# Weight sums paced through the first network, attention traced between its matmuls, split second weights kept by the first token group, block sums in PSUM

## The chip, the cores and the metric

The kernel runs on one core of a Trainium2 chip. The metric is the device time of the whole program in microseconds (us); lower is better. Five engines work side by side: TensorE (PE; its weight loads are PEld), VectorE (DVE), ScalarE (ACT), GpSimd (POOL) and SyncE (SP), which issues most DMAs. Each engine runs its own instructions in a fixed order and waits on semaphores for the others.

## What is computed

```python
attn = masked_softmax(q @ k.T / 8)          # 4 batches, 8 heads, 576 tokens, head size 64
x = (attn @ v) -> (2304, 512)               # window of 32, plain or with dilation 4
xn = x / rms(x) * rms_g                     # first network, width 1536
x = (silu(xn @ w_gate) * (xn @ w_val)) @ w_out
P = sinkhorn(exp(x @ gate2))                # (2304, 8), 8 rounds over rows and columns
for e in range(8):                          # second network, 8 experts, width 1024
    out += P[:, e:e+1] * (relu(x @ w1[e]) @ w2[e])
```

All of it is fp32. The kernel splits each matmul operand into a high part and a remainder (hi, lo) and multiplies hi*hi, hi*lo and lo*hi, so each product takes three matmul passes.

## The kernel before, in words

**First network.** The 2304 tokens are eight blocks of 256 or 320. For a block, `block_att` runs its attention tiles of 128 tokens: scores on PE, softmax on DVE and ACT, then a norm whose power -1/2 is taken on POOL (`rstd`, line 292), then transposes (`psXT`) that give `xn`. `gemm_h` makes one of twelve slices of the hidden layer: PE fills `pg` and `pv`, ACT, DVE and POOL make `h` (lines 473 to 476). `gemm_out` multiplies by `w_out` and stores to `x2d` in HBM. The weights are first unpacked and split on ACT, DVE and POOL (`split_double`, lines 358 to 380); this is done by about 232 us.

**Sums.** The second network multiplies 2x2 blocks with seven products in place of eight (Winograd's form), so it needs sums of weight blocks. `weight_sums` makes them in 64 items, one for each half of `w1` and of `w2` for each of 16 chunks: SP loads 512 KB into one of three buffers (`kbd`, `vbd`, `conv`), one DVE and three POOL operations add blocks, SP stores 512 KB to `sums`. For blocks 2 to 7, `spread` interleaves a side generator with the matmul generators at fixed ratios.

**Second network.** 48 units: three token groups `g` of 768 tokens times 16 chunks (expert and half of its width). A unit has seven steps `s`; step by step, `gemm1(u)` (12 matmuls of 384 columns) alternates with `gemm2(u-1)` (18 matmuls of 256 columns), so a unit of time has 84 + 126 = 210 matmuls. `gemm1` accumulates in three chains of PSUM banks, a, c and b, two banks each out of four: b takes the banks that c leaves, and the next unit's a those that b leaves. After its steps, ACT copies block sums out (`p1`, `pq`, `u4`), DVE adds a bank to them, `direct` makes the hidden blocks a11, a22 and a12 (`h_a`: ACT relu, DVE remainder), and `relu_with` makes four more sums (line 872). `summed` turns those into s2, s4, s3 and s1 (`h_s`: ACT cast, POOL remainder) in the next unit. `gemm2` multiplies the `h` blocks by the split weights and DVE adds the result to `acc`, scaled by the routing weight (line 963).

During unit u, `second_weights(u)` loads four tiles for `w2` (two raw, two of sums) and splits seven blocks (`w_b`, `w_t`: ACT cast, the remainder on DVE for four and on POOL for three), and `first_weights(u+1)` does the same for `w1` (`w_a`, `w_s`, all on POOL). All of them come out of one pool of 20 buffers. This is done anew in each of the three groups, though the weights are the same.

Ahead of the last unit's end of a group, `x_load` and `x_split` prepare the next group's tokens. In units 0 to 2 a side generator does the last gate (`gate`, line 543 on PE) and the Sinkhorn rounds. Instructions stand on an engine in the order that a scheduler in the build makes of the trace order; SP's DMAs are in order too.

## Time and profile before

| | |
|---|---|
| median of three runs | 2268.74 us (2268.07 to 2269.47) |
| profiled execution, its own time | 2270.99 us |
| its span, first to last instruction | 2269.2 us |
| mean granted TensorE clock | 0.960 |
| PE / PEld busy | 2073.0 / 2016.4 us (91%, 89%) |
| DVE / POOL / ACT busy | 1625.0 / 1509.0 / 1135.2 us |

Busy time of PE is the time in which a matmul is in the array, its pipelined end modelled, so 99% is not peak. The idle time of PE and of PEld, and what ended it, tell more. The clock of 1.00 is 2.4 GHz.

### The profile page before, as it was taken

How to read it: one execution, taken by the hardware profiler on the slowest of the kernel's cores; microseconds unless marked ns; L12 is line 12 of the kernel's file. 1: busy time of each engine (PE TensorE's matmuls, PEld its weight loads, DVE VectorE, ACT ScalarE, POOL GpSimd, SP SyncE). 2: the span in 40 equal slices, each digit the busy share in tenths (PEclk: the TensorE clock that was granted, in tenths of full speed). 3: DMA queues.
4: the chain of work that ended last, by engine and by line, in shares of the span. 5: the costliest groups of instructions: out<-in, count | busy, mean ns of one | idle time of the engine just before them, and what ended most of it. 6: DMA issues, size and time to landing. Idle time of an engine off the chain costs nothing.

```text
span 2269.2 us, 42225 instructions
## 1 busy us (share of the span) xinstructions
PE 2073.0 (91%) x16098; PEld 2016.4 (89%) x16098; DVE 1625.0 (72%) x3000; ACT 1135.2 (50%) x2444; POOL 1509.0 (66%) x1351
## 2 busy tenths in 40 slices
...
GB/s 271 170 227 191 269 258 266 174 177 27 53 89 158 91 124 124 130 144 149 149 137 115 143 128 138 140 150 148 124 129 148 121 131 149 149 132 122 128 140 65
DMA packets 161034, 333.48 MB, mean 147 GB/s; under 512 B 12352, under 2 KB 20160, under 8 KB 160832
## 3 DMA queue, kind: packets, MB, share of 16 engines
...
q8 instruction: 126, 2.06, 0.4%
q14 instruction: 76, 0.62, 0.1%
HBM read 287.76 MB, written 42.99 MB: 146 GB/s over the span
## 4 chain that ended last, share of the span: by engine, by line
POOL 23%; PE 22%; DMA 20%; DVE 12%; issue 11%; ACT 4%; POOLq 0%; SPq 0%; DVEq 0%; ACTq 0%
DMA w0r<-in_w 12%; POOL h_s L868 7%; POOL w_a L620 5%; POOL w_s L620 5%; PE ya L935 4%; PE pa L888 3%; PE po L435 3%; PE pv L461 3%; PE pg L461 3%; DVE h_a L860 2%; PE yb L935 2%; DVE w_b L620 2%; POOL w_t L620 2%; DVE acc L963 2%; POOL w_b L620 2%
## 5 line engine op out<-in xcount | busy, mean ns | idle before, releaser
L620 POOL TENSOR_TENSOR w_s<-w0s,w_s 128x512 fp32r<-128x512 f32 x192 | 291.9, 1530 | 12.0 <-ACT w_s L619 12.0
L620 POOL TENSOR_TENSOR w_a<-w0r,w_a 128x512 fp32r<-128x512 f32 x144 | 203.9, 1417 | 141.7 <-ACT w_a L619 126.2
L868 POOL TENSOR_TENSOR h_s<-p,h_s 128x384 fp32r<-128x384 f32 x96 | 125.5, 1323 | 235.1 <-ACT h_s L867 227.7
L963 DVE SCALAR_TENSOR_TENSOR acc<-ya,Pm,acc 128x256 f32<-128x256 f32 x534 | 231.5, 473 | 19.3 <-PE ya L935 16.2
L935 PE MATMUL ya<-w_t,h_s 128*128 128x256 f32 x1728 | 228.6, 285 | 5.9 <-DVE acc L963 5.4
L935 PEld LDWEIGHTS ya<-w_t,h_s 128*128 128x128 f32 x1728 | 222.9, 193 | 7.9 <-DVE acc L963 5.8
L888 PE MATMUL pa<-x_t,w_s 128*128 128x384 f32 x1152 | 223.2, 340 | 3.4 <-ACT p L900 2.4
L461 PE MATMUL pv<-xn,w_v 128*128 128x320 f32 (+1 forms) x1152 | 192.4, 313 | 22.3 <-POOL w_v L374 7.6
L888 PEld LDWEIGHTS pa<-x_t,w_s 128*128 128x128 f32 x1152 | 200.9, 192 | 4.5 <-ACT p L900 2.7
L461 PEld LDWEIGHTS pv<-xn,w_v 128*128 128x128 f32 x1152 | 173.7, 203 | 27.6 <-POOL w_v L374 8.0
L619 ACT CAST w_t<-w1s 128x512 fp32r<-128x512 f32 x192 | 119.0, 621 | 157.5 <-POOL w_s L620 89.5
L461 PE MATMUL pg<-xn,w_g 128*128 128x320 f32 (+1 forms) x1152 | 187.5, 305 | 8.8 <-DVE hf L474 5.7
L435 PE MATMUL po<-h,w_o 128*128 128x320 f32 (+1 forms) x1152 | 182.2, 306 | 7.8 <-DVE partial L446 2.9
L620 DVE TENSOR_TENSOR w_t<-w1s,w_t 128x512 fp32r<-128x512 f32 x96 | 121.2, 1262 | 81.5 <-ACT w_t L619 81.4
L461 PEld LDWEIGHTS pg<-xn,w_g 128*128 128x128 f32 x1152 | 168.4, 196 | 12.4 <-DVE hf L474 6.1
L435 PEld LDWEIGHTS po<-h,w_o 128*128 128x128 f32 x1152 | 165.5, 195 | 12.6 <-DVE partial L446 3.8
L619 ACT CAST w_s<-w0s 128x512 fp32r<-128x512 f32 x192 | 119.2, 621 | 108.0 <-POOL w_a L620 74.5
L476 POOL TENSOR_TENSOR h<-hf,h 128x256 fp32r<-128x256 f32 (+1 forms) x96 | 82.6, 864 | 113.6 <-ACT h L475 113.4
L935 PE MATMUL yb<-w_t,h_s 128*128 128x256 f32 x864 | 131.3, 294 | 21.7 <-POOL h_s L868 21.5
L935 PEld LDWEIGHTS yb<-w_t,h_s 128*128 128x128 f32 x864 | 115.8, 194 | 34.3 <-POOL h_s L868 33.6
L860 DVE SCALAR_TENSOR_TENSOR h_a<-p,h_a 128x384 fp32r<-128x384 f32 x96 | 90.5, 947 | 62.6 <-ACT h_a L859 57.9
L620 POOL TENSOR_TENSOR w_t<-w1s,w_t 128x512 fp32r<-128x512 f32 x96 | 131.7, 1372 | 2.4 <-ACT w_t L619 2.4
(235 smaller groups left out, 5191.7 us busy)
## 6 DMA issues: line engine op xcount, KB each, us to landing
...
```

The costliest lines, as they stand in the source:

```text
L435: nc.tensor.matmul(po[:, :n], lhsT=ow[f][:, a, dc * P : dc * P + P], rhs=hs[blk, f][:, bb, :n], start=k == 0, stop=k == 11,)
L461: nc.tensor.matmul(ps[:, :n], lhsT=w[kt, fg][:, a, fo * P : fo * P + P], rhs=xn[:, kt, bb, :n], start=k == 0, stop=k == 11,)
L476: nc.gpsimd.tensor_tensor(out=h[:, 1, :n], in0=hf, in1=h[:, 0, :n].bitcast(F32), op=ALU.subtract)
L619: nc.scalar.copy(v[:, :, 0, :], src)
L620: lo_eng.tensor_tensor(out=v[:, :, 1, :], in0=src, in1=v[:, :, 0, :].bitcast(F32), op=ALU.subtract)
L860: nc.vector.scalar_tensor_tensor(out=h[:, 1, :], in0=src, scalar=0.0, in1=h[:, 0, :].bitcast(F32), op0=ALU.max, op1=ALU.subtract)
L868: nc.gpsimd.tensor_tensor(out=h[:, 1, :], in0=src, in1=h[:, 0, :].bitcast(F32), op=ALU.subtract)
L888: nc.tensor.matmul(ps, lhsT=w1s[u, a][:, kt, hl, q * P : q * P + P], rhs=xc[b, kt][:, xl, :TH], start=fresh and k == 0, stop=k == 5, skip_ ...
L935: nc.tensor.matmul(ps, lhsT=hh[u, a, q][:, hl, jj * P : jj * P + P], rhs=w2s[u, b][:, q, wl, :], start=fresh and k == 0 and jj != 1, stop= ...
L963: nc.vector.scalar_tensor_tensor(out=dst, in0=ps, scalar=scale, in1=dst, op0=ALU.mult, op1=ALU.add)
```

## The change

Four parts, in the order of the program:

1. `weight_sums` yields twice for each item, is asked for 24 steps in each of blocks 2 to 7 in place of 13, and its additions stand behind the newest `hf` and `h` operations of `gemm_h` on DVE and POOL. `block_att(i+1)` is no longer run ahead of block i's matmuls but is a side generator of their `spread`.
2. `last_gate` takes the place of the last `gate`: all four token tiles are loaded and split first, into tiles of the `h` pool, and the matmuls come five steps later.
3. In group 0, each split `w2` block is also stored to HBM (`split2`, 512 KB). In groups 1 and 2, `second_weights` loads the seven blocks from there and neither loads raw `w2` and its sums nor splits.
4. In `gemm1`, the additions for a11 (step 1) and a12 (step 5) are written back into their PSUM bank, `direct` reads that bank, and ACT copies the sum to `p1` or `pq` afterwards. In step 6 the relu is written into its own bank and two `relu_with` read it there.

```diff
@@ -471,10 +471,11 @@
         h = mpool.tile([P, 2, 320], F32R, tag="h", name=f"h_{blk}_{f}", bufs=5)
         hf = mpool.tile([P, 320], F32, tag="hf", name=f"hf_{blk}_{f}", bufs=2)[:, :n]
         nc.scalar.activation(hf, pg[:, :n], AF.Silu)
-        nc.vector.tensor_tensor(out=hf, in0=pv[:, :n], in1=hf, op=ALU.mult)
+        late_v = nc.vector.tensor_tensor(out=hf, in0=pv[:, :n], in1=hf, op=ALU.mult)
         nc.scalar.copy(h[:, 0, :n], hf)
-        nc.gpsimd.tensor_tensor(out=h[:, 1, :n], in0=hf, in1=h[:, 0, :n].bitcast(F32), op=ALU.subtract)
+        late_g = nc.gpsimd.tensor_tensor(out=h[:, 1, :n], in0=hf, in1=h[:, 0, :n].bitcast(F32), op=ALU.subtract)
         hs[blk, f] = h
+        marks["late"] = (late_v, late_g)
         yield
 
     pending = []
@@ -565,6 +566,8 @@
         for w in range(2) for ch in range(NCH)
     }
 
+    split2 = [dram.tile([7, P, 1024], F32, name=f"split2_{ch}", tag=f"split2_{ch}") for ch in range(NCH)]
+
     def raw_of(w, ch):
         e, c = divmod(ch, 2)
         return w1[e, :, 512 * c : 512 * c + 512] if w == 0 else w2[e, 512 * c : 512 * c + 512, :]
@@ -584,6 +587,10 @@
         yield
         for i, (w, ch, k) in enumerate(items):
             nxt = load(i + 1) if i + 1 < len(items) else None
+            yield
+            late = ExitStack()
+            for m in marks["late"]:
+                late.enter_context(tc.issue_after(m.ins))
             x11, x12, x21, x22 = (t[:, a, 256 * c : 256 * c + 256] for a in range(2) for c in range(2))
             if w == 0:
                 nc.gpsimd.tensor_tensor(out=x22, in0=x12, in1=x22, op=ALU.add)
@@ -595,6 +602,7 @@
                 nc.vector.tensor_tensor(out=x12, in0=x22, in1=x12, op=ALU.subtract)
                 nc.gpsimd.tensor_tensor(out=x22, in0=x11, in1=x22, op=ALU.subtract)
                 nc.gpsimd.tensor_tensor(out=x21, in0=x21, in1=x22, op=ALU.add)
+            late.close()
             nc.sync.dma_start(sums[w, ch][:, k, :], t.rearrange("p i n -> p (i n)"))
             t = nxt
             yield
@@ -618,7 +626,7 @@
         v = t.rearrange("p k (s n) -> p k s n", s=2)
         nc.scalar.copy(v[:, :, 0, :], src)
         lo_eng.tensor_tensor(out=v[:, :, 1, :], in0=src, in1=v[:, :, 0, :].bitcast(F32), op=ALU.subtract)
-        return v
+        return t, v
 
     def first_weights(u):
 
@@ -626,19 +634,27 @@
         yield
         yield
         for m, src in (("a11", a11), ("a12", a12), ("s2", s2), ("s3", s3), ("s1", s1), ("a22", a22), ("s4", s4)):
-            w1s[u, m] = split_block(f"w1_{u}_{m}", src, nc.gpsimd)
+            w1s[u, m] = split_block(f"w1_{u}_{m}", src, nc.gpsimd)[1]
             yield
 
     def second_weights(u):
 
+        g, ch = units[u]
+        names = ("b11", "b21", "t2", "t3", "t1", "t4", "b22")
+        if g > 0:
+            for j, m in enumerate(names):
+                t = wx.tile([P, 2, 512], F32R, tag="w", name=f"w2_{u}_{m}")
+                nc.sync.dma_start(t.rearrange("p k n -> p (k n)").bitcast(F32), split2[ch][j])
+                w2s[u, m] = t.rearrange("p k (s n) -> p k s n", s=2)
+                yield
+            return
         b11, b12, b21, b22, t1, t3, t4, t2 = blocks_of(1, u)
         yield
         yield
         yield
-        for j, (m, src) in enumerate(
-            (("b11", b11), ("b21", b21), ("t2", t2), ("t3", t3), ("t1", t1), ("t4", t4), ("b22", b22))
-        ):
-            w2s[u, m] = split_block(f"w2_{u}_{m}", src, nc.gpsimd if j % 2 else nc.vector)
+        for j, (m, src) in enumerate(zip(names, (b11, b21, t2, t3, t1, t4, b22))):
+            t, w2s[u, m] = split_block(f"w2_{u}_{m}", src, nc.gpsimd if j % 2 else nc.vector)
+            nc.sync.dma_start(split2[ch][j], t.rearrange("p k n -> p (k n)").bitcast(F32))
             yield
 
 
@@ -787,12 +803,14 @@
     ready = {2: (0,), 3: (1,), 4: (2,), 6: (3,)}
     sgen1 = weight_sums()
     for i in range(2, 8):
+        sides = [(some(sgen1, 24), 24)]
         if i < 7:
-            run(block_att(i + 1))
-            spread(moe1_chunks([(i, 0), (i, 1), (i, 2)]), 34, [(some(sgen1, 13), 13), *((later(g), 34) for g in ready.get(i, ()))])
+            sides.append((block_att(i + 1), 7 * len(blocks[i + 1][2])))
+            sides += [(later(g), 34) for g in ready.get(i, ())]
         else:
-            run(sgen1)
-            spread(moe1_chunks([(i, 0), (i, 1), (i, 2)]), 34, [(tail(), 34), (later(4), 34)])
+            sides += [(tail(), 34), (later(4), 34)]
+        spread(moe1_chunks([(i, 0), (i, 1), (i, 2)]), 34, sides)
+    run(sgen1)
 
     ph1.close()
     psum_a.close()
@@ -807,9 +825,42 @@
     ones = acp.tile([P, P], F32, name="ones")
     nc.gpsimd.memset(ones, 1.0)
 
+    def last_gate():
+
+        blk = NT // TH - 1
+        xg = [hp_.tile([P, 2, TH], F32R, tag="h", name=f"xg_{kt}") for kt in range(4)]
+        for kt in range(4):
+            st = stg.tile([P, 512], F32, tag="st", name=f"sx_{blk}_{kt}", bufs=3)[:, :TH]
+            nc.sync.dma_start(st, x2d[kt, :, TH * blk : TH * blk + TH])
+            nc.scalar.copy(xg[kt][:, 0, :], st)
+            nc.gpsimd.tensor_tensor(out=xg[kt][:, 1, :], in0=st, in1=xg[kt][:, 0, :].bitcast(F32), op=ALU.subtract)
+            if kt % 2:
+                yield
+        for _ in range(5):
+            yield
+        pl = ps_o.tile([P, 512], F32, tag="o", name="pl_last")
+        for k in range(8):
+            kt, hl = divmod(k, 2)
+            nc.tensor.matmul(
+                pl[:16, :TH], lhsT=wg[:, kt].rearrange("p s e -> p (s e)"), rhs=xg[kt][:, hl, :], start=k == 0, stop=k == 7
+            )
+        yield
+        lg = stg.tile([16, 512], F32, tag="st", name="lg_last", bufs=3)
+        nc.scalar.copy(lg[:, :TH], pl[:16, :TH])
+        for _ in range(2):
+            yield
+        ptl = ps_o.tile([P, 512], F32, tag="o", name="ptl_last")
+        nt = TH // P
+        for j in range(nt):
+            nc.tensor.transpose(ptl[:, j * 16 : j * 16 + 16], lg[:, j * P : j * P + P], id16)
+        nc.vector.tensor_copy(
+            L2[:, nt * blk : nt * blk + nt, :], ptl[:, : nt * 16].rearrange("p (t e) -> p t e", e=16)
+        )
+        yield
+
     def side():
 
-        yield from gate(NT // TH - 1)
+        yield from last_gate()
         nc.vector.tensor_tensor(out=Pm, in0=L2[:, :, 0:8], in1=L2[:, :, 8:16], op=ALU.add)
         gm = acp.tile([P, 2], F32, name="gm")
         nc.vector.tensor_reduce(out=gm[:, 0:1], in_=Pm.rearrange("p t e -> p (t e)"), axis=AX.X, op=ALU.max)
@@ -898,17 +949,22 @@
                     tag = {0: "p1", 2: "pq", 4: "u4"}[s]
                     t[tag, q] = temp(tag, u, q)
                     nc.scalar.copy(t[tag, q], ps)
-                if s in (1, 4, 5):
-                    m, tag, src = {1: ("a11", "p1", "c"), 4: ("a22", "u4", "b"), 5: ("a12", "pq", "b")}[s]
+                if s in (1, 5):
+                    m, tag = {1: ("a11", "p1"), 5: ("a12", "pq")}[s]
                     x = t[tag, q]
-                    nc.vector.tensor_tensor(out=x, in0=bank[src, q][:, :TH], in1=x, op=ALU.add)
-                    direct(u, m, q, x)
+                    nc.vector.tensor_tensor(out=ps, in0=ps, in1=x, op=ALU.add)
+                    direct(u, m, q, ps)
+                    nc.scalar.copy(x, ps)
+                if s == 4:
+                    x = t["u4", q]
+                    nc.vector.tensor_tensor(out=x, in0=bank["b", q][:, :TH], in1=x, op=ALU.add)
+                    direct(u, "a22", q, x)
                 if s == 6:
                     r = t["r", q] = temp("r", u, q)
-                    nc.scalar.activation(r, ps, AF.Relu)
+                    nc.scalar.activation(ps, ps, AF.Relu)
                     c11, c22, c21 = (t[n, q] for n in ("p1", "u4", "pq"))
-                    relu_with(c22, c22, r, ALU.add)
-                    relu_with(r, c11, r, ALU.subtract)
+                    relu_with(c22, c22, ps, ALU.add)
+                    relu_with(r, c11, ps, ALU.subtract)
                     relu_with(c11, c11, c22, ALU.subtract)
                     relu_with(c21, c21, c11, ALU.add)
             yield
```

The scheduler's order changes with it. POOL, second half of block 0 and 1's hidden slices: `h_4` is a slice's remainder, `m_o`, `w_o` and `m_g` are first-network weights being unpacked, `kbd` and `vbd` are sums. Before:

```order
L476 TENSOR_TENSOR h_7_1524<-hf_7_1525,h_7_1524 128x256
L374 TENSOR_SCALAR w_o_1287<-m_o_1270 128x256
L369 TENSOR_TENSOR m_o_1309<-m_o_1309,sd_o_1307 128x256
L378 TENSOR_TENSOR w_o_1287<-m_o_1270,w_o_1287 128x256
L596 TENSOR_TENSOR kbd<-kbd 128x256
L476 TENSOR_TENSOR h_4_1556<-hf_4_1557,h_4_1556 128x320
L378 TENSOR_TENSOR w_o_1306<-m_o_1309,w_o_1306 128x256
L369 TENSOR_TENSOR m_o_1309<-m_o_1309,sd_o_1327 128x256
L378 TENSOR_TENSOR w_o_1287<-m_o_1270,w_o_1287 128x256
L369 TENSOR_TENSOR m_o_1309<-m_o_1309,sd_o_1327 128x256
L589 TENSOR_TENSOR vbd<-vbd 128x256
L378 TENSOR_TENSOR w_o_1306<-m_o_1309,w_o_1306 128x256
```

and now:

```order
L476 TENSOR_TENSOR h_7_1540<-hf_7_1541,h_7_1540 128x256
L369 TENSOR_TENSOR m_g_1733<-m_g_1733,sd_g_1731 128x256
L378 TENSOR_TENSOR w_o_1322<-m_o_1325,w_o_1322 128x256
L369 TENSOR_TENSOR m_g_1733<-m_g_1733,sd_g_1731 128x256
L378 TENSOR_TENSOR w_o_1322<-m_o_1325,w_o_1322 128x256
L476 TENSOR_TENSOR h_4_1572<-hf_4_1573,h_4_1572 128x320
L374 TENSOR_SCALAR w_o_1342<-m_o_1325 128x256 x2
L378 TENSOR_TENSOR w_o_1342<-m_o_1325,w_o_1342 128x256 x2
L369 TENSOR_TENSOR m_g_1733<-m_g_1733,sd_g_1751 128x256 x2
L374 TENSOR_SCALAR w_g_1750<-m_g_1733,cst 128x256 x2
L369 TENSOR_TENSOR conv<-conv,sd_g_0_1770 128x256
L369 TENSOR_TENSOR conv<-conv,sd_g_1_1780 128x256
```

The additions on `kbd` and `vbd` are gone from here; the first now stand behind slice 24.

POOL, first token group, start of unit 10's weights: `h_8_*` are unit 8's summed blocks, `w1_10_*` the next split `w1`. Before:

```order
L868 TENSOR_TENSOR h_8_s2_0_11429<-p1_8_0_11045,h_8_s2_0_11429 128x384
L868 TENSOR_TENSOR h_8_s2_1_11432<-p1_8_1_11054,h_8_s2_1_11432 128x384
L620 TENSOR_TENSOR w1_10_a11_11508<-w0r_10_0_11443,w1_10_a11_11508 128x2x256
L868 TENSOR_TENSOR h_8_s4_0_11496<-pq_8_0_11173,h_8_s4_0_11496 128x384
L868 TENSOR_TENSOR h_8_s4_1_11499<-pq_8_1_11181,h_8_s4_1_11499 128x384
L868 TENSOR_TENSOR h_8_s3_0_11502<-r_8_0_11372,h_8_s3_0_11502 128x384
L868 TENSOR_TENSOR h_8_s3_1_11505<-r_8_1_11384,h_8_s3_1_11505 128x384
L868 TENSOR_TENSOR h_8_s1_0_11556<-u4_8_0_11277,h_8_s1_0_11556 128x384
L868 TENSOR_TENSOR h_8_s1_1_11559<-u4_8_1_11289,h_8_s1_1_11559 128x384
L620 TENSOR_TENSOR w1_10_a12_11537<-w0r_10_1_11445,w1_10_a12_11537 128x2x256
L620 TENSOR_TENSOR w2_9_b21_11562<-w1r_9_1_11437,w2_9_b21_11562 128x2x256
```

and now:

```order
L919 TENSOR_TENSOR h_8_s2_0_11540<-p1_8_0_11145,h_8_s2_0_11540 128x384
L919 TENSOR_TENSOR h_8_s2_1_11543<-p1_8_1_11154,h_8_s2_1_11543 128x384
L919 TENSOR_TENSOR h_8_s4_0_11609<-pq_8_0_11276,h_8_s4_0_11609 128x384
L919 TENSOR_TENSOR h_8_s4_1_11612<-pq_8_1_11284,h_8_s4_1_11612 128x384
L919 TENSOR_TENSOR h_8_s3_0_11615<-r_8_0_11483,h_8_s3_0_11615 128x384
L919 TENSOR_TENSOR h_8_s3_1_11618<-r_8_1_11495,h_8_s3_1_11618 128x384
L919 TENSOR_TENSOR h_8_s1_0_11670<-u4_8_0_11384,h_8_s1_0_11670 128x384
L919 TENSOR_TENSOR h_8_s1_1_11673<-u4_8_1_11396,h_8_s1_1_11673 128x384
L628 TENSOR_TENSOR w1_10_a11_11621<-w0r_10_0_11554,w1_10_a11_11621 128x2x256
L628 TENSOR_TENSOR w1_10_a12_11651<-w0r_10_1_11556,w1_10_a12_11651 128x2x256
L628 TENSOR_TENSOR w2_9_b21_11676<-w1r_9_1_11548,w2_9_b21_11676 128x2x256
```

The remainder `w1_10_a11` stood between `h_8_s2` and the six others and now stands behind all eight. In groups 1 and 2, `a11` and `a12` both stand in that place.

PE, first token group, where unit 10 begins: `ya_8`, `ya_9` are gemm2 results, `pa_10_0` and `pa_10_1` the two banks of chain a. Before, with the semaphore of the engine that each row waits for:

```order
L935 MATMUL ya_8_1_11452<-w2_8_b22_11322,h_8_s4_1_11499 128x256 x3
L888 MATMUL pa_10_0_11784<-x_0_b11_0_7545,w1_10_a11_11508 128x384 [waits DVE_49]
L888 MATMUL pa_10_0_11784<-x_0_b11_0_7545,w1_10_a11_11508 128x384 x2
L888 MATMUL pa_10_0_11784<-x_0_b11_1_7548,w1_10_a11_11508 128x384 x3
L888 MATMUL pa_10_1_11793<-x_0_b11_0_7545,w1_10_a11_11508 128x384 [waits DVE_49]
L888 MATMUL pa_10_1_11793<-x_0_b11_0_7545,w1_10_a11_11508 128x384 x2
L888 MATMUL pa_10_1_11793<-x_0_b11_1_7548,w1_10_a11_11508 128x384 x3
L935 MATMUL ya_9_0_11824<-w2_9_b11_11534,h_9_a11_0_11482 128x256 [waits DVE_49]
```

and now:

```order
L991 MATMUL ya_8_1_11563<-w2_8_b22_11430,h_8_s4_1_11612 128x256 x3
L991 MATMUL ya_9_0_11946<-w2_9_b11_11647,h_9_a11_0_11593 128x256 [waits DVE_49]
L939 MATMUL pa_10_0_11906<-x_0_b11_0_7561,w1_10_a11_11621 128x384 [waits Activation_49]
L939 MATMUL pa_10_0_11906<-x_0_b11_0_7561,w1_10_a11_11621 128x384
L939 MATMUL pa_10_0_11906<-x_0_b11_0_7561,w1_10_a11_11621 128x384 [waits Pool_49]
L939 MATMUL pa_10_0_11906<-x_0_b11_1_7564,w1_10_a11_11621 128x384 x3
L991 MATMUL ya_9_0_11946<-w2_9_b11_11647,h_9_a11_0_11593 128x256 x2
L991 MATMUL ya_9_0_11946<-w2_9_b11_11647,h_9_a11_1_11605 128x256 x3
L991 MATMUL ya_9_0_11946<-w2_9_b11_11647,h_9_a11_0_11593 128x256
L939 MATMUL pa_10_1_11915<-x_0_b11_0_7561,w1_10_a11_11621 128x384 [waits Activation_49]
L939 MATMUL pa_10_1_11915<-x_0_b11_0_7561,w1_10_a11_11621 128x384 x2
L939 MATMUL pa_10_1_11915<-x_0_b11_1_7564,w1_10_a11_11621 128x384 x3
```

Both banks waited for DVE (the addition that last read them) and now wait for ACT (the copy of that sum to `pq`); one matmul of `ya_9` moved ahead of `pa_10_0` and six between it and `pa_10_1`.

## Rows read from the trace of the kernel before

**Rows 1.** Nine windows: length, busy us of each engine, PEclk, DMA share, GB/s.

```profile
45.00:250.00 205.00, 151.75 (x1297) 140.05 (x1298) 174.36 (x346) 97.01 (x250) 165.50 (x218) 0.84 0.60 209
250.00:480.00 230.00, 203.28 (x2281) 194.06 (x2281) 89.98 (x189) 78.23 (x169) 125.61 (x167) 0.93 0.69 235
480.00:690.00 210.00, 209.87 (x2114) 205.49 (x2112) 71.48 (x153) 77.92 (x172) 64.89 (x70) 1.00 0.24 79
690.00:875.00 185.00, 154.12 (x986) 147.68 (x987) 137.33 (x254) 94.12 (x198) 111.67 (x88) 0.93 0.34 118
875.00:1210.00 335.00, 327.53 (x2283) 322.91 (x2282) 268.47 (x494) 186.41 (x390) 252.77 (x193) 1.00 0.42 141
1210.00:1330.00 120.00, 100.72 (x655) 98.39 (x655) 100.31 (x145) 65.12 (x140) 82.17 (x61) 0.91 0.37 126
1330.00:1728.00 398.00, 390.59 (x2719) 386.15 (x2718) 321.05 (x586) 222.28 (x464) 300.49 (x229) 1.00 0.41 140
1728.00:1847.00 119.00, 102.65 (x642) 100.28 (x642) 98.01 (x146) 64.77 (x139) 81.86 (x61) 0.89 0.37 127
1847.00:2217.00 370.00, 361.68 (x2519) 357.58 (x2518) 292.95 (x538) 206.70 (x430) 283.48 (x216) 1.00 0.41 136
```

**Rows 2.** Waits of PEld in 875:1210: total us, times, longest.

```profile
PEld yb L935 <- POOL h_s L868: 10.4, 20, 1.7
```

**Rows 3.** Waits of PEld in 1330:1728.

```profile
PEld yb L935 <- POOL h_s L868: 9.8, 18, 2.1
```

**Rows 4.** Waits of PEld in 1847:2217.

```profile
PEld yb L935 <- POOL h_s L868: 12.1, 19, 2.1
```

**Rows 5.** Waits of PE in 1210:1330.

```profile
PE pa L888 <- ACT u L900: 5.6, 1, 5.6
PE yc L935 <- DVE acc L963: 4.8, 2, 4.6
PE ya L935 <- DVE acc L963: 4.5, 1, 4.5
```

**Rows 6.** Waits of PE in 690:875.

```profile
PE pl L543 <- ACT g L539: 11.1, 3, 7.6
...
PE pl L543 <- POOL g L540: 3.3, 3, 2.1
```

**Rows 7.** POOL at line 592, one of three additions of an item, by stage.

```profile
0.00:250.00 250.00, 10.01 (x12) 0.87 0.65 217
250.00:480.00 230.00, 14.46 (x19) 0.93 0.69 235
```

**Rows 8.** POOL timeline, 228:240: start us, us, instruction, [idle before, releaser].

```profile
236.38 0.72 POOL L589 TENSOR_TENSOR vbd<-vbd 128x256 f32<-128x256 f32 x1 [4.40 <-DMA vbd<-in_w]
```

**Rows 9.** Lines by form, 1330:1728: busy us, mean ns | idle before.

```profile
L620 POOL TENSOR_TENSOR w_t<-w1s,w_t 128x512 fp32r<-128x512 f32 x24 | 32.1, 1339 | 0.0
...
L620 DVE TENSOR_TENSOR w_t<-w1s,w_t 128x512 fp32r<-128x512 f32 x24 | 29.8, 1244 | 23.6 <-ACT w_t L619 23.6
...
L860 DVE SCALAR_TENSOR_TENSOR h_a<-p,h_a 128x384 fp32r<-128x384 f32 x26 | 23.7, 915 | 17.3 <-ACT h_a L859 15.7
...
L872 DVE SCALAR_TENSOR_TENSOR u<-u,r 128x384 f32<-128x384 f32 x26 | 13.2, 547 | 0.0
...
L904 DVE TENSOR_TENSOR p<-pc,p 128x384 f32<-128x384 f32 x26 | 13.1, 543 | 0.0
```

**Rows 10.** PE timeline, 1035:1044, unit 10.

```profile
1040.08 2.25 PE L888 MATMUL pb<-x_t,w_s 128*128 128x384 f32 x12
```

**Rows 11.** DVE timeline, 1035:1041.

```profile
1038.60 1.33 DVE L860 SCALAR_TENSOR_TENSOR h_a<-p,h_a 128x384 fp32r<-128x384 f32 x1 [1.44 <-ACT h_a L859]
```

**Rows 12.** ACT timeline, 1036:1042.

```profile
1037.53 0.62 ACT L619 CAST w_a<-w0r 128x512 fp32r<-128x512 f32 x1 [0.95 <-DMA w0r<-in_w]
...
1038.48 0.91 ACT L867 CAST h_s<-pq 128x384 fp32r<-128x384 f32 x2
```

**Rows 13.** Windows, 250:300.

```profile
250.00:300.00 50.00, 43.45 (x541) 41.49 (x541) 22.34 (x48) 18.98 (x42) 29.04 (x40) 0.91 0.84 286
```

## The prediction

> **What bounds the kernel now.** I first cut the span into stages and read the busy time of each engine in each [rows 1]. Then I read, stage by stage, the waits of PE and of its weight loads, and last the lines by form and single instructions for prices.
>
> The reader is to see five kinds of stretch in [rows 1].
>
> - *Steady second network* (875 to 1210, 1330 to 1728, 1847 to 2217). A unit has 210 matmuls, so these hold 2283/210 = 10.9, 12.9 and 12.0 units of 30.8, 30.7 and 30.8 us, at clock 1.00. Almost all the loss is one wait: the load of `h_s` as weights of `yb` waits for POOL's remainder, 10.4 + 9.8 + 12.1 = 32.3 us [rows 2 to 4]. Without it a unit is (335 - 10.4)/10.9 = 29.9 us. That is my floor.
> - *Group boundaries* (1210 to 1330, 1728 to 1847). 655 and 642 matmuls are 3.12 and 3.06 units, 93 and 91 us at the floor, and take 120 and 119: 27 and 28 us lost. DVE is busy 100 of 120 us, more than anywhere else in the second network, and PE waits for its `acc` and for ACT's `u` [rows 5]. The clock is 0.91 and 0.89, a mean over stretches at 2.4 and at 1.2 GHz; a matmul takes 100.72/655 = 0.154 us against 327.53/2283 = 0.143, so some 7 of the 27 us are the clock's.
> - *Start of the second network* (690 to 875). 986 matmuls are 4.7 units or 140 us; it takes 185, so 45 are lost. The last gate's `pl` waits 14.4 of them, for ACT and POOL to split its tokens one tile at a time [rows 6].
> - *First network, early* (45 to 250). PE idles 53 us at clock 0.84, while DVE is busy 85% and POOL 81%.
> - *First network, later.* 250 to 480 leaves PE 26.7 us idle at clock 0.93; 480 to 690 leaves it nothing (209.87 of 210). The sums sit in the earlier two: line 592, which serves the 32 items of `w1`, runs 12 times before 250, 19 times before 480 and once later [rows 7]. So about 24, 38 and 2 of the 64 items lie there.
>
> **The change, part by part.**
>
> *Paced sums.* Each item has three POOL additions of 10.01/12 = 0.83 us [rows 7], so 24 items are 60 us of POOL's 165 before 250, and by the DVE price of a 384-column operation [rows 9], scaled to 256 columns, at most 0.55 us x 24 = 13 us of DVE. They also hold up what stands behind them: one `vbd` addition kept POOL waiting 4.40 us for its load [rows 8]. Removing them lets the weight unpacking, bound by DVE and POOL, end earlier. Bounds: nothing, if the unpacking is bound by DVE's own 160 us, to 45 of the 53 idle us. I take 20, nearer the DVE end, since DVE was the busier. The program spreads the 64 items evenly over blocks 2 to 7, from about 250 to 660: 64 x 230/410 = 36 in 250 to 480, as many as now, and 28 after 480, some 25 more than now. Those meet a PE that never idles. With POOL busy 65 and DVE 71 of 210 us, their 25 x 2.5 = 62 us of POOL fit. By 250 to 480's own idle time, 26.7 us for 38 items, they would cost 25 x 0.7 = 18. Attention now traced among the matmuls can move the idle time either way; I take -5 for all that follows 250, with -28 (that 18, and 10 more if `xn` comes late) to +27 (all idle time of 250 to 480 gone). **Phase 1: +15.**
>
> *Last gate.* Its four splits now run ahead, and the matmuls come five steps later, so the 14.4 us of waits go. Those waits also keep the clock at 0.93 and push the Sinkhorn rounds; DVE also loses the 0.37 us per `h_a` told below. I take 18, from 5 (the wait moves to `lg`) to 30 of the 45. **Start: +18.**
>
> *Split w2 kept.* In groups 1 and 2 a unit loses four DVE remainders of 1.24 us (5.0), three POOL remainders of 1.34 (4.0) and seven ACT casts of 0.62 (4.3) [rows 9, 12], for 32 units. POOL, now 300/12.9 = 23 us a unit, is what `h_s` waits for. Moreover the order shows `a11` behind all eight `h_s` instead of ahead of six: it waits for a load (its cast waited 0.95 us for `w0r` [rows 12]) and takes 1.3 us, as long as the longest waits of 1.7 and 2.1. With both, the `yb` wait has no cause left but the relus' own lateness. I take 27 of the 32.3 us, from 10 (group 0's alone) to all and a little more, 36. **Steady: +27.**
>
> At a boundary some 2.2 of the 3.1 units (an estimate) lie in the new group and lose 5.0 us of DVE each: 11 us. With 3.1 x 1.5 of the next part this is 16 of DVE's 100 us, and PE's shorter idle time gives back part of the 7 us of clock. I take half of the 55, 28; from 8 (DVE's casts wait for `x` loads instead) to 45. **Boundaries: +28.**
>
> Its price is DMA. In group 0 seven stores of 512 KB add 3.7 MB to 141 GB/s x 30.8 us = 4.3 MB: 8.0 MB in 30 us is 267 GB/s, against 286 GB/s at a share of 0.84 that the chip does from 250 to 300 [rows 13]. It fits with little left; the loads of `w0r` and of raw w2 share queues with the stores. I take -3, bounds 0 and -64 (rival 3). In groups 1 and 2 seven reads replace four.
>
> *Block sums in PSUM.* `h_a` with two SBUF operands takes 915 ns, with outliers like 1.33 [rows 9, 11]; the `p` addition, which reads a bank, takes 543 and the SBUF-only `u` 547 [rows 9]. `u`'s operands lie in SBUF too, so the excess of 0.37 us belongs to the moment at which `h_a` runs, with POOL's remainders beside it; whether a bank as operand avoids it, no row shows of `h_a` itself. I take all of it for the four `h_a` a unit that now read a bank, 1.5 us of DVE, since no operation on a bank shows it; the other bound is nothing. It counts only where DVE bounds, at the boundaries above. The Trainium skill (VectorE: DVE Perf Modes, "The TRN2 errata — SBUF-src ops pay a fixed extra latency per instruction") states the reverse: 120 fixed cycles from PSUM against 58 from SBUF. By it eight operations a unit would each lose 62 cycles or 65 ns, 0.5 us a unit, an estimate from that page; a boundary would then get 11 - 1.6 = 9.4 of DVE's 100 us back and not 16, in proportion 17 us for the 28, and the time would be 2201. The trace disagrees, with 543 against 547 ns.
>
> The new waits: ACT copies four sums a unit, at 0.91/2 = 0.46 us [rows 12], 1.8 us on an ACT that is busy 222/12.9 = 17 us of 30.7. Until then the bank stays held. For `pb` the copy `p1` stands behind both relus and six casts. In unit 10 the second relu ran behind the `w_a` cast that starts at 1037.53 [rows 12]; that cast now stands behind the copy, so the relu can end by 1037.5, six casts at 0.46 by 1040.3 and the copy by 1040.8. `pb` started at 1040.08 [rows 10], and six `yb` matmuls of some 0.12 us (0.143 is the mean of both widths) now stand ahead of it, which makes that 1040.8. So it is just met. For the next `pa` the copy `pq` in group 0 stands behind w2's last cast; I estimate 0.3 us in each of 16 units. **New waits: -5, from 0 to -137 (rival 1).**
>
> Sum: 15 + 18 + 27 + 28 - 5 - 3 = 80. The profiled execution took 2270.99 us, 0.1% over the median of 2268.74. 2271 - 80 = 2191, and by the median 2189: **I forecast 2190 us.**
>
> **Rivals.**
>
> 1. *Banks held by copies (slower).* If ACT's casts start only behind the second `h_a` remainder, which ended at 1039.93 [rows 11], then six casts (2.5 us) and the copy end at 1042.9, 2.8 us after `pb` was due [rows 10]. In 48 units that is 137 us: 2190 + 137 = 2327. It decides from 80/48 = 1.7 us a unit on. Against it: the casts need neither remainder. For it: the program makes each copy wait for the remainder of its bank, and in group 0 the second copy stands behind a `w_a` cast that waits for a load. Chance 0.08.
> 2. *The paced sums only move the idle time.* The first 250 us stay bound by unpacking and the 25 late items cost their 18: 2190 + 15 + 18 = 2223. For it: 480 to 690 has no PE idle time to give. Against: POOL is busy 31% there. Chance 0.15.
> 3. *Stores make group 0 wait for DMA.* At the 235 GB/s that 250 to 480 reached [rows 1], 8.0 MB take 34 us, 4 us over the floor, and 16 units give +64: 2254; half that at the rate between. Chance 0.10.
> 4. *The splits were hidden anyway.* DVE's saved work frees nothing on PE's path, `yb` still waits for late relus, and the last gate's wait moves on to the Sinkhorn rounds: about 2268. Chance 0.05.
>
> The forecast itself has 0.62, and its own range is 2155 to 2225.
>
> **How the numbers follow.** A measurement here can tell 0.2%, 4.5 us. Forecast, rivals 2 and 3 are faster: 0.87; rival 4 the same: 0.05; rival 1 slower: 0.08. The range goes down to the case in which the boundaries and the first network after 250 both give their upper bounds, 2190 - 17 - 32 = 2141, and up to rival 3 almost whole. It leaves out rivals 1 and 4, the end of rival 3 and what may lie below, about 0.08 + 0.05 + 0.03 + 0.04.
>
> **What would show it.** Right: `yb` no longer waits for `h_s`, steady windows at 29.9 to 30.1 us a unit; no `pl` waits; boundary windows shorter by about 14 us each at a clock nearer 1.00; the last unpacking addition well before 232 us; `h_a` from a bank at 0.55 us; group 0 near 265 GB/s. Wrong: `pa` or `pb` waiting for the ACT copies by over 1.7 us a unit; PE idle in 480 to 690; `w0r` landing late in group 0; boundary windows as long as before, which would mean that what they wait for is not DVE's amount of work.

## The result, and the profile after

The changed kernel took 2106.74 us (median of four runs, 2105.13 to 2107.08) against 2268.4 us; the ratio is 0.929, with an interval of 0.927 to 0.930. The forecast was 2190 us with a range of 2140 to 2250: the direction was right, and the gain of 162 us was twice the 80 us forecast and 33 us past the range's end.

The profiled execution has a span of 2103.3 us and a mean granted clock of 0.987. Its windows, cut at the stages' own ends, in the columns of [rows 1]:

```profile
45.00:250.00 205.00, 182.22 (x1808) 167.72 (x1807) 157.38 (x355) 109.89 (x283) 133.53 (x179) 0.92 0.40 137
250.00:480.00 230.00, 221.98 (x2485) 213.70 (x2469) 98.23 (x207) 86.63 (x183) 132.45 (x175) 0.99 0.69 237
480.00:632.00 152.00, 148.06 (x1431) 144.14 (x1430) 61.60 (x124) 55.00 (x123) 85.71 (x102) 1.00 0.59 207
632.00:789.00 157.00, 143.55 (x956) 137.33 (x955) 127.06 (x250) 100.63 (x216) 109.54 (x88) 0.99 0.66 240
789.00:1088.00 299.00, 298.67 (x2102) 296.66 (x2100) 252.66 (x451) 186.71 (x400) 232.16 (x180) 1.00 0.74 263
1088.00:1218.00 130.00, 122.97 (x842) 120.72 (x843) 94.65 (x183) 76.09 (x168) 80.23 (x66) 0.99 0.68 241
1218.00:1573.00 355.00, 355.00 (x2518) 355.00 (x2517) 236.00 (x492) 186.72 (x396) 203.04 (x180) 1.00 0.58 195
1573.00:1699.00 126.00, 122.81 (x846) 121.72 (x845) 86.05 (x174) 72.59 (x159) 74.40 (x62) 0.97 0.61 210
1699.00:2054.00 355.00, 355.00 (x2518) 355.00 (x2517) 235.96 (x492) 186.74 (x396) 202.98 (x180) 1.00 0.58 197
```

The reader is to see the clock near 1.00 nearly everywhere, PE without idle time in the steady windows, and the DMA share of 0.74 in group 0, where the stores of split w2 are. The last unpacking addition on POOL begins at 195.8 us, in place of about 231:

```profile
L378 POOL TENSOR_TENSOR w_o<-conv,w_o x16: 724/782/932, 69.1 to 195.8; 128x256 fp32r<-128x256 f32 x16
```

From here on I use lengths between first matmuls, which need no windows: a block lasts from its first `pg` to the next block's, a unit from its first `pa` to the next unit's. The table has them for all kernels, from one profiled execution each (bl.: blocks 0-1, 2-4 and 5-7 of the first network; u.: units 0-4; the mean unit of three steady parts; the two boundaries, units 15-18 and 31-34; the last unit, to its last matmul), with the medians and ratios of the timed runs. Where a run leaves a stretch as it was, its length repeats within a few us: 206 to 212 for blocks 0 and 1, 242 to 248 for 2 to 4, 147 to 150 for a boundary.

| kernel | median us | ratio (interval) | bl. 0-1 | 2-4 | 5-7 | u. 0-4 | 5-14 | 15-18 | 19-30 | 31-34 | 35-46 | 47 |
|---|---|---|---|---|---|---|---|---|---|---|---|---|
| before | 2268 | | 210 | 244 | 205 | 179 | 30.78 | 148 | 30.67 | 149 | 30.87 | 48 |
| the whole change | 2107 | 0.929 (0.927-0.930) | 173 | 215 | 210 | 157 | 29.91 | 130 | 29.63 | 125 | 29.63 | 45 |
| only_paced | 2220 | 0.978 (0.975-0.982) | 174 | 220 | 211 | 176 | 30.84 | 150 | 30.84 | 149 | 30.75 | 48 |
| late_only | 2222 | 0.981 (0.977-0.984) | 173 | 222 | 220 | 180 | 31.10 | 148 | 30.75 | 149 | 30.55 | 48 |
| no_late | 2170 | 0.958 (0.955-0.961) | 209 | 247 | 206 | 157 | 29.94 | 130 | 29.63 | 124 | 29.63 | 45 |
| only_attention | 2283 | 1.006 (1.004-1.009) | 209 | 245 | 206 | 192 | 31.27 | 149 | 30.62 | 149 | 30.99 | 48 |
| no_attention | 2114 | 0.933 (0.931-0.936) | 173 | 219 | 216 | 159 | 29.91 | 128 | 29.63 | 125 | 29.63 | 45 |
| no_loads | 2235 | 0.987 (0.985-0.989) | 207 | 222 | 204 | 175 | 30.69 | 147 | 30.48 | 150 | 30.67 | 48 |
| only_gate | 2261 | 0.997 (0.995-0.999) | 206 | 248 | 205 | 168 | 30.87 | 150 | 30.64 | 148 | 30.78 | 48 |
| only_split | 2202 | 0.970 (0.967-0.973) | 212 | 242 | 204 | 187 | 29.85 | 135 | 29.63 | 125 | 29.63 | 46 |
| split_dve | 2225 | 0.983 (0.981-0.985) | 209 | 243 | 205 | 185 | 29.88 | 136 | 30.32 | 134 | 30.42 | 46 |
| split_pool | 2224 | 0.981 (0.978-0.985) | 210 | 243 | 204 | 188 | 29.84 | 141 | 30.19 | 129 | 30.16 | 46 |
| only_psum | 2238 | 0.987 (0.984-0.989) | 210 | 246 | 204 | 170 | 31.00 | 135 | 30.88 | 134 | 30.77 | 47 |
| no_psum | 2128 | 0.940 (0.938-0.942) | 174 | 214 | 211 | 175 | 29.70 | 134 | 29.63 | 127 | 29.63 | 46 |
| order_only | 2258 | 0.997 (0.995-0.999) | 209 | 243 | 204 | 177 | 31.08 | 139 | 30.94 | 142 | 31.11 | 49 |
| order_both | 2221 | 0.980 (0.976-0.984) | 207 | 247 | 204 | 178 | 29.73 | 142 | 29.63 | 143 | 29.63 | 49 |

Of the span's 166 us the first network gave 62 (the second network's first `pa` starts at 632.2 in place of 693.9) and the second 104. The experiments go by these two.

### The profile page after: what moved, and what is told of

The parts are those of the page before. It is cut to its first block, busy times and chain, and to the rows that moved or that the text cites. A ratio compares the mean times of both kernels' runs of the same rounds, so it can differ in the third digit from the quotient of the medians.

```text
span 2103.3 us, 42498 instructions
## 1 busy us (share of the span) xinstructions
PE 2021.4 (96%) x16098; PEld 1977.4 (94%) x16098; DVE 1413.4 (67%) x2872; ACT 1101.8 (52%) x2412; POOL 1288.3 (61%) x1255
## 4 chain that ended last, share of the span: by engine, by line
PE 76%; DVE 9%; DMA 5%; POOL 4%; issue 3%; ACT 2%; SPq 1%; DVEq 0%; POOLq 0%; ACTq 0%
PE ya L991 17%; PE pa L939 16%; PE yb L991 9%; PE pb L939 8%; PE po L435 5%; PE pg L461 5%; PE pv L461 5%; PE yc L991 4%; PE pc L939 4%; DMA sx<-x2d 2%; DMA xr<-x2d 1%; DVE h_a L911 1%; DVE acc L1019 1%; POOL h_s L919 1%; DMA kbd<-in_kt 1%
## 5 line engine op out<-in xcount | busy, mean ns | idle before, releaser
L628 POOL TENSOR_TENSOR w_s<-w0s,w_s 128x512 fp32r<-128x512 f32 x192 | 268.3, 1401 | 66.2 <-ACT w_s L627 66.1
L919 POOL TENSOR_TENSOR h_s<-p,h_s 128x384 fp32r<-128x384 f32 x96 | 105.1, 1102 | 311.2 <-ACT h_s L918 298.0
L628 POOL TENSOR_TENSOR w_a<-w0r,w_a 128x512 fp32r<-128x512 f32 x144 | 195.4, 1361 | 79.8 <-ACT w_a L627 77.4
L461 PEld LDWEIGHTS pv<-xn,w_v 128*128 128x128 f32 x1152 | 166.7, 194 | 16.5 <-DVE hf L474 4.4
L1019 DVE SCALAR_TENSOR_TENSOR acc<-yb,Pm,acc 128x256 f32<-128x256 f32 x270 | 114.8, 474 | 95.7 <-PE yb L991 95.6
L919 POOL TENSOR_TENSOR h_s<-pq,h_s 128x384 fp32r<-128x384 f32 x96 | 96.8, 1030 | 59.9 <-ACT h_s L918 59.9
L991 PE MATMUL yb<-w_t,h_a 128*128 128x256 f32 x864 | 124.5, 282 | 0.3 <-DVE acc L1019 0.3
L627 ACT CAST w_a<-w0r 128x512 fp32r<-128x512 f32 x144 | 89.4, 621 | 64.7 <-PE ya L991 17.6
L991 PE MATMUL yb<-w_t,h_s 128*128 128x256 f32 x864 | 120.6, 283 | 0.7 <-ACT h_s L918 0.7
L939 PE MATMUL pa<-x_b,w_a 128*128 128x384 f32 x576 | 114.7, 342 | 5.8 <-ACT pq L957 4.0
```

Of the source, the lines that this page charges most:

```text
L461: nc.tensor.matmul(ps[:, :n], lhsT=w[kt, fg][:, a, fo * P : fo * P + P], rhs=xn[:, kt, bb, :n], start=k == 0, stop=k == 11,)
L627: nc.scalar.copy(v[:, :, 0, :], src)
L628: lo_eng.tensor_tensor(out=v[:, :, 1, :], in0=src, in1=v[:, :, 0, :].bitcast(F32), op=ALU.subtract)
L919: nc.gpsimd.tensor_tensor(out=h[:, 1, :], in0=src, in1=h[:, 0, :].bitcast(F32), op=ALU.subtract)
L939: nc.tensor.matmul(ps, lhsT=w1s[u, a][:, kt, hl, q * P : q * P + P], rhs=xc[b, kt][:, xl, :TH], start=fresh and k == 0, stop=k == 5, skip_ ...
L991: nc.tensor.matmul(ps, lhsT=hh[u, a, q][:, hl, jj * P : jj * P + P], rhs=w2s[u, b][:, q, wl, :], start=fresh and k == 0 and jj != 1, stop= ...
```

## Experiments on the first network

**Paced sums alone, and attention alone.** The first takes part 1 without its attention:

```diff
-            spread(..., [(some(sgen1, 13), 13), ...])
+            spread(..., [(some(sgen1, 24), 24), ...])
...
+            for m in marks["late"]:
+                late.enter_context(tc.issue_after(m.ins))
```

> Of part 1 only the paced sums (two steps an item, 24 a block, additions behind the newest slice); attention is still traced ahead of each block, the rest as before. The whole change made blocks 0 and 1 shorter by 16.6 and 20.7 us, blocks 2 to 4 by 29.3 together, blocks 5 and 6 longer by 6.3. Theory (POOL freed early): blocks 0 and 1 are shorter by about 37 us as in the whole change, blocks 2 to 4 by 0 to 10, 5 and 6 longer by 5 to 10; 2268 - 35 = 2233. Rival (the sums were what PE waited for everywhere): all 61 us of the first network, 2207. Rival (attention between the matmuls did it): under 10 us, over 2258.

Blocks 0 and 1 became 36 us shorter, blocks 2 to 4 became 24 us shorter, and blocks 5 to 7 became 6 us longer: nearly the whole gain of the first network. That lies between the two readings that I had written down. The second takes only the attention:

```diff
-            run(block_att(i + 1))
+            sides = [(some(sgen1, 13), 13), (block_att(i + 1), 7 * len(blocks[i + 1][2]))]
```

> Of part 1 only the attention of the next block traced among the matmuls; sums at 13 steps a block as before. Theory (each half has its own stretch): blocks 0 and 1 unchanged, blocks 2 to 4 shorter by 20 to 29 us, since their waits for psX and xs (11 us) and the clock of 0.93 go; about 2244. Rival (attention gives nothing without the paced sums, since DVE and POOL stay full): within 5 us of 2268.

The first network is unchanged to 1 us, as the rival had it. The total is 16 us longer (1.004 to 1.009 times), which neither reading had; 12 of these lie in units 0 to 4 of the profiled run, which take 192 us here and 175 to 180 in the other runs that change only the first network. Why, no run shows.

**No attention.** The whole change with `run(block_att(i + 1))` again:

```diff
-            sides.append((block_att(i + 1), 7 * len(blocks[i + 1][2])))
+            run(block_att(i + 1))
```

> The whole change with the attention of the next block traced ahead of each block again. Theory (from the run with attention alone, which gave the first network nothing, and the one with the paced sums, whose blocks 2 to 4 took 5 us more than the whole change's): 4 to 8 us longer, about 2113. Rival (attention needs the paced sums to help, and together they give what the single parts leave open): 15 us or more, over 2121. Rival (it costs, as it did alone): 2106 or less.

2114.5 us, 8 us over the whole change: 10 us in the first network. The attention is worth that with paced sums, and nothing without.

**Marks or pace.** Part 1 has two means: additions behind the newest slice (the marks), and 24 steps a block. `no_late` is the whole change without the marks, `late_only` the kernel before with the marks alone:

```diff
-            for m in marks["late"]:
-                late.enter_context(tc.issue_after(m.ins))
```

> The whole change without one thing: the additions of the sums no longer stand behind the newest slice's hf and h operations; the 24 steps a block stay. In this build's order POOL's first additions stand at place 29 again, as before the change, and not at 158. Theory (the marks did it, the pace alone lets the scheduler pull the sums ahead): the first network loses what the paced sums gave, 50 to 60 us, and the second network is unchanged: about 2160. Rival (the pace of 24 steps did it): under 10 us, at most 2117.

> The kernel before with the marks alone: additions behind the newest slice, but 13 steps a block and the rest of the items run ahead of block 7, as before. Theory (marks): blocks 0 and 1 shorter by 35 us, as in the run with the paced sums, blocks 2 to 6 by 10 to 20 together, and a loss at block 7, whose slices wait behind the items left over: about 2225. Rival (pace): 2260 to 2268.

Without the marks the first network is as long as before (209, 247, 206), whatever the pace; with them alone blocks 0 and 1 are at 173 and 2 to 4 at 222. The marks did it. The pace of 24 only takes back most of what late_only loses in blocks 5 to 7 (220 us, against 205 before and 211 in only_paced). That loss lies in blocks 5 and 6, and not in block 7 as I had expected.

Why blocks 2 to 4 gain is what I had missed, since about as many sums lie there as before: 41 items in the kernel before and 38 in late_only, each counted where its last addition begins. POOL's waits in these blocks (245 to 488 us; total, times, longest), in the kernel before:

```profile
POOL conv L589 <- DMA conv<-in_w: 21.7, 7, 5.3
...
POOL conv L594 <- DMA conv<-in_w: 11.8, 5, 4.8
POOL kbd L594 <- DMA kbd<-in_w: 10.7, 4, 5.7
POOL vbd L594 <- DMA vbd<-in_w: 10.5, 5, 3.7
...
POOL kbd L589 <- DMA kbd<-in_w: 6.0, 4, 3.2
POOL vbd L589 <- DMA vbd<-in_w: 5.4, 4, 3.2
```

and in late_only (206 to 429 us), all of sums waiting for loads:

```profile
POOL vbd L598 <- DMA vbd<-in_w: 4.8, 2, 3.3
POOL kbd L593 <- DMA kbd<-in_w: 4.5, 1, 4.5
...
POOL kbd L598 <- DMA kbd<-in_w: 2.0, 1, 2.0
POOL conv L598 <- DMA conv<-in_w: 1.3, 2, 1.2
POOL conv L593 <- DMA conv<-in_w: 1.3, 1, 1.3
```

POOL stood still for 66 us at additions whose load had not landed, and for 14 with the marks. POOL works in order, so the slices' remainders (`h`), the gates' (`g`) and `rstd` that stand behind such an addition are late with it. To test whether it is this wait and not the amount or place of the additions, one more run left the loads out:

```diff
+            if i < 3:
                 nc.sync.dma_start(t, raw_of(w, ch)...)
```

> The kernel before without the loads of the sums' items after the third: additions and stores run as before, at the same early places, on what lies in the buffers, so the sums are not those of the weights. Theory (POOL stands still at an addition that waits for its load, 66 us in blocks 2 to 4, and what is queued behind it is late): blocks 2 to 4 take about 222 us together, as in the run with the marks alone, in place of 244, and blocks 0 and 1 are 5 to 15 shorter. Rival (the amount of additions before 250 us, or their place): blocks 2 to 4 within 5 us of 244. Against a third reading, that it is the traffic, stands the run with the marks alone, which has the same traffic there.

Blocks 2 to 4 took 222 us, as long as late_only's. But the run does not keep the additions at their places: without loads to wait for, the build's order puts them earlier. The last additions of 22, 15 and 3 items begin in blocks 2, 3 and 4, against 16, 18 and 7 before and 12, 13 and 13 in late_only. Nor does POOL stop waiting at them. It now waits for the stores that empty their buffers (244 to 466 us):

```profile
POOL conv L590 <- DMA sums<-conv: 16.0, 7, 5.4
POOL conv L595 <- DMA sums<-conv: 15.5, 7, 3.7
```

With two smaller rows these waits are 34 us, so 31 of the 66 us went here and 52 in late_only, and each time the three blocks gained the same 22 us. What the two runs show is this. The amount of sums in these blocks is not the cause, since it is about the same in all three kernels (41, 40 and 38 items). Traffic is not the cause either, since late_only moves 241 GB/s there against 230 before. In both runs POOL stands less at its additions, which makes this wait the likely cause; but their places changed too, so it is not shown by itself, and no run gives its price.

Blocks 0 and 1 took 207 us, no less than in other runs that leave them alone, where I had expected 5 to 15 us of gain. There the marks take the additions away, and with the loads alone gone the additions are still there; so it is mostly the additions themselves. Which engine's (POOL's three or DVE's one) was not separated.

## Experiments on the second network

**Split w2 alone.** Part 3 of the diff, of which these lines are the core:

```diff
+            nc.sync.dma_start(split2[ch][j], t...)
...
+                nc.sync.dma_start(t..., split2[ch][j])
```

> Only part 3 (split w2 stored in group 0, loaded in groups 1 and 2). In this build's order POOL's a11 remainder of the next w1 stands behind all eight h_s in group 0, as in the whole change, though POOL has as much to do there as before. Theory (order): steady units of group 0 fall from 30.8 to about 29.9 us all the same, those of groups 1 and 2 to 29.6 or 29.7, and the two boundaries give 35 of the whole change's 42 us; about 2268 - 75 = 2193. Rival (amount of POOL's work): group 0 stays at 30.8, and only groups 1 and 2 gain, 2203. Rival (boundaries were freed by bank operands): boundaries give under 15 us, 2215.

Steady units took 29.85 and 29.63 us, and the boundaries were 38 us shorter, as the order reading has it. The total of 2202 is 9 us over that reading, mostly in units 0 to 4, which took 187 us in place of 179. Group 0 gained although POOL has the same work there and stores were added.

**Block sums alone.** Part 4 of the diff, of which these lines are the core:

```diff
-                    direct(u, m, q, x)
+                    direct(u, m, q, ps)
+                    nc.scalar.copy(x, ps)
```

> Only part 4 (block sums in PSUM). In this build's order the a11 remainder still stands ahead of six h_s. Theory (order): yb still waits for h_s, steady units 30.4 to 30.8 us in all three groups, boundaries shorter by 3 to 5 us each; about 2258. Rival (DVE's and POOL's contention over SBUF was it): units at 29.9 us, boundaries shorter by 10 us each, about 2215. Rival 1 of the prediction (banks held by the copies): PE waits over 1.7 us a unit for them, over 2280.

Total 2238, between the readings. Steady units stayed at 30.8 to 31.0 as the order reading had it, but not for its reason. PEld's waits from 890 to 1170:

```profile
PEld pa L888 <- ACT pq L906: 7.3, 9, 0.8
PEld pb L888 <- ACT p L906: 3.6, 9, 0.7
```

`yb`'s wait was gone, and the banks held by the copies took its place: 10.9 us in 9 units. This is rival 1's wait, at 1.2 us a unit instead of 2.8. In the whole change it shrinks to

```profile
PEld pa L939 <- ACT pq L957: 2.3, 10, 0.4
```

from 789 to 1088. The boundaries gained 28 us, more than the rival's 20.

**Order.** To test the order by itself, a11's remainder on POOL was put behind the newest `h_s`, and nothing else:

```diff
+        late = behind("hs") if "_a11" in name and "hs" in marks else ExitStack()
         lo_eng.tensor_tensor(...)
```

> The kernel before, and only POOL's remainder of a11 is made to stand behind the newest h_s, in all three groups; no work is added or removed. Theory (order): the waits of yb for h_s go, units 5 to 14, 19 to 30 and 35 to 46 take 29.7 to 30.0 us in place of 30.8, boundaries stay at 148 to 149, in all about 2268 - 32 = 2236. Rival (amount of POOL's and DVE's work): units stay at 30.6 or more, within 6 us of 2268.

My reading fell: units took 31.0 us. Yet the boundaries became 17 us shorter, which neither reading had. The trace says why the units did not gain. ACT's rows in that kernel, in one unit:

```profile
1034.93 0.63 ACT L619 CAST w_a<-w0r 128x512 fp32r<-128x512 f32 x1 [1.23 <-DMA w0r<-in_w]
1035.46 0.51 ACT L861 ACTIVATE h_a<-p 128x384 fp32r<-128x384 f32 x1
1035.88 0.91 ACT L869 CAST h_s<-pq 128x384 fp32r<-128x384 f32 x2
```

The six casts of `h_s` stand on ACT behind a11's cast, which waits for its load: they start late, whatever POOL does. So the next run moved the whole of a11, cast and remainder:

```diff
+        late = behind("hs_a", "hs_g") if "_a11" in name and "hs_g" in marks else ExitStack()
         nc.scalar.copy(v[:, :, 0, :], src)
         lo_eng.tensor_tensor(...)
```

Before, the `w_a` cast stands ahead of all six `h_s` casts [rows 12]. Now ACT does, in the same unit:

```profile
1030.30 0.91 ACT L869 CAST h_s<-pq 128x384 fp32r<-128x384 f32 x2
1031.12 0.93 ACT L869 CAST h_s<-r 128x384 fp32r<-128x384 f32 x2
1031.95 0.61 ACT L620 CAST w_a<-w0r 128x512 fp32r<-128x512 f32 x1
1032.47 0.92 ACT L869 CAST h_s<-u 128x384 fp32r<-128x384 f32 x2
```

The cast stands behind four of the six and waits for nothing.

> The kernel before, and a11 as a whole (ACT's cast, which waits for the load of w0r, and POOL's remainder) stands behind the newest h_s on its engine; nothing else is changed. Theory (the wait of yb is made on two engines: ACT's cast of a11 stands ahead of the six h_s casts and makes them 0.9 to 1.9 us late, POOL's remainder adds 1.3): yb waits no more than 2 us in ten units, steady units take 29.7 to 30.0 us in all three groups, about 2268 - 30 = 2238, less what the boundaries give as in the run before (18). Rival (POOL's and DVE's amount of work after all): units stay at 30.6 or more.

Units took 29.73, 29.63 and 29.63 us, with no operation added or taken away, and `yb` waits nowhere from 890 to 1170. PE in this kernel:

```profile
890.00:1170.00 280.00, 280.00 (x1982) 279.85 (x1982) 237.06 (x424) 162.40 (x339) 227.44 (x172) 1.00 0.40 138
```

So the order alone can give the steady units their 38 us. POOL is busier here (227 of 280) than before (252.77 of 335 in [rows 1]); its work was not the limit.

In group 0 the whole change has this order: from 789 to 1088 ACT casts a11 behind the `h_s`, and stands 0.1 us in all ahead of its `w_a` casts, against 9.0 from 875 to 1210 before. In groups 1 and 2 that holds for POOL alone. There ACT casts a11, and now a12 too, ahead of the six `h_s`:

```profile
1401.54 0.49 ACT L910 ACTIVATE h_a<-pc 128x384 fp32r<-128x384 f32 x1 [1.09 <-DVE pc L955]
1401.92 0.61 ACT L627 CAST w_a<-w0r 128x512 fp32r<-128x512 f32 x1
1402.96 0.92 ACT L918 CAST h_s<-pq 128x384 fp32r<-128x384 f32 x2
```

Of ACT's 20.8 us of waits ahead of `w_a` casts from 1218 to 1573 none is put down to `w0r`, and the relu beside the cast waits for DVE. What made these casts early enough, the work and loads that are gone or the new order of the rest, was not separated.

**The boundaries.** Part 3 alone, with DVE's lost work given back in groups 1 and 2 on a scratch tile that nothing reads, and then POOL's:

```diff
+                if j % 2 == 0:
+                    for k in range(2):
+                        nc.vector.tensor_tensor(out=scr, in0=..., in1=..., op=ALU.subtract)
```

> Part 3 alone, and DVE gets back in groups 1 and 2 what it lost: for each of the four blocks two subtractions of 128x256 from the loaded tile into a scratch tile that nothing reads. Theory (the boundaries are bound by DVE's amount of work): units 15 to 18 and 31 to 34 go back from 134.9 and 124.6 us to 142 or more each, while the steady units stay at 29.7 to 29.9: about 2225. Rival (POOL's work or the order freed them): boundaries within 3 us of 134.9 and 124.6, about 2203.

> Part 3 alone, and POOL gets back in groups 1 and 2 what it lost: for each of the three blocks two subtractions of 128x256 from the loaded tile into a scratch tile that nothing reads. Giving DVE its work back cost 0.7 us in each steady unit and 10 of the 38 us that the boundaries had won. Theory (at the boundaries DVE's operations on SBUF are held by POOL's, so it is POOL's work that counts): units 15 to 18 and 31 to 34 go back from 134.9 and 124.6 us to 142 or more each. Rival (neither amount counts there, the order and the missing ACT casts do): within 4 us each. Steady units: 29.6 to 29.8 if the order alone decides, 30.3 or more if POOL's amount does.

Each gives back 10.5 of the 38 us (270.0 against 259.5 for both boundaries; split_dve nearly all of it at the second, 133.7 against 124.6), and 13 us come by the order alone, in order_both. So no reading holds alone, and that the three add up (34 of 38) is not shown. Nor are the 10.5 us shown to be the price of DVE's or POOL's amount of work, since the operations on the scratch tile wait for the loads of `split2` at the head of their queue. Here are those of split_dve from 1350 to 1650, about ten steady units, then of split_pool in the same stretch, then of split_dve from 1185 to 1320, its first boundary:

```profile
DVE scr L645 <- DMA w_t<-split: 5.9, 9, 1.3
```

```profile
POOL scr L645 <- DMA w_b<-split: 8.8, 8, 2.6
```

```profile
DVE scr L645 <- DMA w_t<-split: 5.7, 2, 3.7
```

Each run also costs 0.5 to 0.8 us in a steady unit, of the size of these waits (0.6 us a unit on DVE, 0.9 on POOL). There it is not the amount: POOL is busy 228 of 300 us in split_pool and 241 in order_both, DVE 251 in split_dve and 257 in order_both, and order_both's units take 29.63 us. The ACT casts that are gone were not given back in any run.

**Without block sums, and the last gate alone.** Part 4 left out of the whole change (the first two lines stand for it), and part 2 added to the kernel before (the last line):

```diff
-                    direct(u, m, q, ps)
+                    direct(u, m, q, x)
...
+        yield from last_gate()
```

> The whole change without part 4. Theory (split w2 and bank operands free the same DVE at the boundaries, so they overlap): units 15 to 18 and 31 to 34 take 3 to 8 us more than the whole change's 255 together, units 0 to 4 some 9 more, the rest equal: about 2120. Rival (they add): 28 us more at the boundaries, about 2143. Rival (the copies cost PE more than the banks give): under 2106.

> Only part 2 (the last gate's four splits first, its matmuls five steps later). Theory: the 14 us of waits of pl go, units 0 to 4 take 160 to 168 us in place of 179, the rest as before: about 2254. Rival (the wait moves on, to lg or to the Sinkhorn rounds): within 5 us of 2268. The start varied from 170 to 192 us in runs that did not touch it, so the waits of pl decide, not the total.

Without part 4 the boundaries are 6 us longer, so parts 3 and 4 overlap there, and units 0 to 4 are 18 us longer, twice what I expected; steady units of group 0 are 0.21 us shorter, about the wait for the copies above (2.3 us in ten units). The gate alone: of the waits of `pl` 0.2 us are left, and units 0 to 4 take 168 us; but PE then waits for `u`, `r` and `pq` (6.0, 5.5 and 5.3 us), so 11 of the 14.4 us come through in the profiled run, 6 in the median.

## Why the prediction was wrong

| term | predicted | measured | by |
|---|---|---|---|
| blocks 0, 1 | +20 | +37 | first matmuls |
| all later blocks | -5 | +24 | first matmuls, and 1 us ahead of block 0 |
| start, units 0-4 | +18 | +22 | 179.2 to 156.7 |
| steady units | +27 | +36, and 3 in the last unit | the means |
| boundaries | +28 | +42 | 297.6 to 255.2 |
| new waits, DMA | -8 | -3 | contained in the steady units: 16 x 0.21 |

The step that failed is "I take -5 for all that follows 250". It priced the sums by their additions' busy time and by PE's idle time for an item, and found as many items before and after. Measured are +24 us, near the upper bound of +27 that I had set and not chosen. late_only shows what gave it: the marks alone shorten blocks 2 to 4 by 22 us, with about as many sums in the same blocks. The likely way is a wait that the working left out. [rows 8] showed an addition on POOL waiting 4.40 us for its load, and the next row of that view is a norm's power that stood behind it:

```profile
237.06 0.70 POOL L292 TENSOR_TENSOR rstd<-rstd,neghalf 128x2 f32<-128x2 f32 x1
```

I took this as one instance. It was a pattern of 66 us in blocks 2 to 4, and the marks left 14. That this wait by itself is worth the 22 us stays open, since no_loads took away only half of it and moved the additions. The feared loss behind 480 us was 6.

The second step is a size: blocks 0 and 1 gave 37 us, not 20. "Nearer the DVE end" was the wrong choice, since the bound of 45 was nearer; the marks alone give all of it (late_only).

The third is a size whose reason was partly wrong. For the steady units I named two causes, POOL's smaller load and a11 behind `h_s` on POOL. order_both shows that the order alone can give all of it, and order_only that POOL's half of the order gives none while ACT's cast waits for its load ahead of `h_s`. [rows 12] had ACT's half in plain sight: the `w_a` cast waits for `w0r`, and the `h_s` casts come behind it. My floor of 29.9 was also too high: it is 29.63.

The fourth is a size too. For the boundaries I took the steady window's price of 915 ns for `h_a`, and took a gain for four operations a unit that move to a bank. There are eight, as my own sentence on the Trainium skill's figure counted: four of `relu_with` as well. And at a boundary they cost more. DVE in the kernel before was busy 11.97 of 12 us there (columns as in [rows 1]; the second stretch follows):

```profile
1286.00:1298.00 12.00, 7.46 (x59) 7.25 (x57) 11.97 (x13) 5.62 (x13) 9.70 (x7) 0.98 0.27 89
1298.00:1308.00 10.00, 10.00 (x67) 10.00 (x68) 5.29 (x12) 2.88 (x7) 0.04 (x1) 0.85 0.70 242
```

Three DVE rows of the first stretch, and POOL beside them:

```profile
1287.19 1.64 DVE L872 SCALAR_TENSOR_TENSOR p<-p,u 128x384 f32<-128x384 f32 x1
1288.76 1.65 DVE L872 SCALAR_TENSOR_TENSOR r<-p,r 128x384 f32<-128x384 f32 x1
...
1293.20 0.54 DVE L872 SCALAR_TENSOR_TENSOR pq<-pq,p 128x384 f32<-128x384 f32 x1
```

```profile
1286.81 1.61 POOL L620 TENSOR_TENSOR w_s<-w0s,w_s 128x512 fp32r<-128x512 f32 x1
1288.38 1.61 POOL L620 TENSOR_TENSOR w_a<-w0r,w_a 128x512 fp32r<-128x512 f32 x1
1289.96 1.34 POOL L868 TENSOR_TENSOR h_s<-p,h_s 128x384 fp32r<-128x384 f32 x1
1291.26 1.61 POOL L620 TENSOR_TENSOR w_t<-w1s,w_t 128x512 fp32r<-128x512 f32 x1
1293.90 1.30 POOL L868 TENSOR_TENSOR h_s<-p,h_s 128x384 fp32r<-128x384 f32 x1 [1.04 <-ACT h_s L867]
```

The first two DVE rows end 0.4 us behind the end of the POOL row that ran when they began, as if they stood still until POOL was done; the third began and ended while POOL was idle, and took 0.54 us. Behind these rows the `acc` additions were late, and PE waited and came back at a lower clock, granted 0.85 over the next 10 us, a mean of stretches at 1.2 and at 2.4 GHz:

```profile
1297.99 3.71 PE L935 MATMUL ya<-w_b,h_s 128*128 128x256 f32 x18 [4.54 <-DVE acc L963]
```

18 matmuls in 3.71 us, against 2.31 elsewhere in this unit: 0.206 us each, and 0.128. After the change (DVE by form, 1088 to 1218):

```profile
L911 DVE SCALAR_TENSOR_TENSOR h_a<-u,h_a 128x384 fp32r<-128x384 f32 x8 | 7.9, 991 | 0.8 <-ACT h_a L910 0.8
...
L923 DVE SCALAR_TENSOR_TENSOR u<-u,pa 128x384 f32<-128x384 f32 x10 | 5.5, 545 | 0.9 <-ACT pa L964 0.8
L923 DVE SCALAR_TENSOR_TENSOR r<-p,pa 128x384 f32<-128x384 f32 x10 | 5.4, 545 | 0.0
...
L911 DVE SCALAR_TENSOR_TENSOR h_a<-pb,h_a 128x384 fp32r<-128x384 f32 x9 | 4.9, 548 | 0.7 <-ACT h_a L910 0.6
```

In these rows an operation with a bank as operand takes 545 to 548 ns, and `h_a<-u`, still on SBUF, 991. So what the prediction took without a row of `h_a` itself, that a bank avoids the excess, holds. The Trainium skill (SBUF — State Buffer, "Who interferes with whom") says the same: a DVE instruction with two SBUF inputs contends with a GpSimd instruction that reads SBUF, and one with at most one does not, outside the 2-port perf modes. The trace agrees, with 991 ns against 545 to 548. Of the Trainium skill's other rule, which the prediction cites, the extra fixed cycles from PSUM, nothing shows here either: 545 against the 547 of [rows 9].

Right were: the DMA of group 0, forecast at 267 GB/s and measured at 263, without a wait for it among PE's; the unpacking's earlier end; and that the banks held by the copies would just be met. The last gate's term came out near (18 and 22), but partly by luck. "No `pl` waits" did not come true in the whole change, where PE still waits 5.0 of the 14.4 us (632 to 789):

```profile
PE pl_last L844 <- POOL xg L836: 3.6, 3, 2.0
...
PE pl_last L844 <- ACT xg L835: 1.4, 1, 1.4
```

And without the block sums units 0 to 4 take 175 us (no_psum), so most of the 22 us needs them too, where I had put only a small part of the term on them. Rival 1's wait exists in only_psum and all but goes in the whole change; what takes it away was not tested. Rival 2 fell: blocks 5 to 7 lost 6 us, and the first network gained 62 all the same. Rival 3 fell with the 29.91 us of group 0. Rival 4 fell with all of it.

Still open: what POOL's wait in blocks 2 to 4 is worth by itself; what units 0 to 4 hang on, which took 170 to 192 us in runs that did not touch the gate; and how the boundaries' gain divides among order, DVE and POOL, since each part alone gives much of it (split w2 38 us, block sums 28, POOL's order 17) and the whole change 42.
